# A Fourier-matrix aside rank of six instead of three, and a search over three hundred orders instead of ninety, in an attention and Fourier-mixing kernel

## The chip, the cores and the metric

The kernel runs on one core of one Trainium2 chip. Its time is the device time of one execution in microseconds (us). Before the change three runs took 2828.16, 2829.85 and 2834.0 us, so the median is 2829.85 us.

## The reference, cut to what matters

```python
# A: attention, 32 heads of 32, S = 2048, D = 1024, full softmax
qkv = (x @ wqkv).reshape(B, S, 3, 32, 32).transpose(2, 0, 3, 1, 4)
scores = einsum("bhqd,bhkd->bhqk", q, k) * 32 ** -0.5
o = einsum("bhqk,bhkd->bhqd", softmax(scores), v)
a = o.transpose(0, 2, 1, 3).reshape(B, S, D) @ wo
# B: Fourier mixing, real part of DFT_seq(DFT_hidden(x))
re, im = einsum("bsd,ed->bse", x, hid_re), einsum("bsd,ed->bse", x, hid_im)
y = einsum("ts,bse->bte", seq_re, re) - einsum("ts,bse->bte", seq_im, im)
return concatenate([a, y], axis=-1)
```

The kernel first multiplies B's x by the sequence matrices (cosine `ct[0]`, then sine `ct[1]`, the second Fourier matrix) and then by the hidden ones.

## The kernel before

**Work of the matrix engine.** Every float32 product outside attention is made of three matmuls of 128x128 by 128x512: both operands are split into a high and a low part (a "piece", `halves`, lines 535 to 548: a cast on ACT or DVE, L542 or L544, and a subtraction on POOL or DVE, L547), and high*high, low*high and high*low are added up in one PSUM bank. On top of that the products follow a seven-product scheme, so pieces are sums or differences of blocks (line 522 makes such a sum from two loads). All these matmuls (line 457) are called fills; there are 6528 of them. Attention runs beside them, head by head: scores in pairs of matmuls (L1896, tile `psS`), whose row maxima DVE takes (L1902) and whose exponentials ACT sums (L1905); the scores transposed (L2018, tile `psT`), whose exponentials ACT writes as `pt` (L2022); and `pt` times v (L2037, "PV"), 20 or 24 matmuls of each of 96 PV steps.

**What sets the order.** The program first only records operations, each with an engine (sometimes a second engine it could go to), a rank, what it waits for and which buffer of a ring it takes. A planner (`Plan`, `run`) then walks through a modelled time with costs per operation. For ACT, DVE, POOL and SP it takes the ready operation with the lowest rank; for PE it chooses between the next fill (in the one fixed order of `fills`) and the next step of scores, transposed scores and PV. The rank is mostly `seq()`, the number of product groups recorded so far, plus 10, 20 or 25 for an operation's second choice. What comes out is each engine's fixed list of instructions. On the chip each engine goes down its list and waits at each instruction for that one's inputs.

**The search.** Eight numbers steer the choices (LATE, NEAR, PATIENCE, STOCK, SFIRST, SST, LEAD, RES). The planner is run once with set values, then TRIALS times with drawn ones: every third time a fresh draw, otherwise the best so far with two numbers redrawn; a draw is kept if the modelled end is earlier. The best is then emitted. The seed is fixed.

**Pieces made aside.** Some pieces of the two big products with the sequence matrices are made early, beside the projection of q, k and v, and stored to DRAM (`ha_d`) for later. `aside_c` (line 1306) makes such pieces of B's x from loads `c<-in_xb` (L1327): a sum (L1333), a cast (L1334), a subtraction (L1335) and two stores (L1336). It makes 16, eight each for two products, and gives all their operations `rank = seq() + LATER`. `aside` makes others, among them sums of blocks of the Fourier matrices (loads L1373 `slot<-in_ct`, sum L1375, store L1381 `tg_d`, `tb_d`), at `seq() + AHEAD`, and the change leaves that rank alone. While q, k and v are projected, aside pieces, loads for the projection (L506: `raw<-in_wqk`, `raw<-tx_d`) and the first heads share SP's one list of DMA issues.

```python
pp, p, i = todo_c.pop(0)
rank = seq() + LATER
...
for n in range(TRIALS):
    if n % 3 == 0:
        some = {k: rng.uniform(*v) for k, v in SPAN.items() if rng.random() < 0.6}
    else:
        some = {**best, **{k: rng.uniform(*SPAN[k]) for k in rng.sample(list(SPAN), 2)}}
    t = run(True, **some)
    if t < shortest:
        best, shortest = some, t
```

Of the kernel before, what the change touches and what calls it, by code (L numbers as in the profile page):

```python
# [253 lines left out]
def kernel(  # L254
# [137 lines left out]
    LATE = 0.25  # L392
    HB = 0
    ACAST = 0.6
    TRIALS = 90
    RES = 700
    SST = 13
    LEAD = 3.0
# [901 lines left out]
    def put_b(r, pp, j):  # L1300
        return pp, "b", r, j
# [37 lines left out]
    kept_a = {}  # L1339

    todo_a = [put_b(1, pp, j) for pp in ORDER if pp in (5, 6, 7, 4) for j in range(16)]
    AHEAD, EACH, LATER = 2, 1, 3

    todo_t = [put_b(0, 4, j) for j in range(16)]

# [843 lines left out]
    best, shortest = {}, run(True)  # L2189
    for n in range(TRIALS):  # L2190
        if n % 3 == 0:
# [41 lines left out]
```

## Time and profile before

| | before |
|---|---|
| median of three runs | 2829.85 us |
| the profiled execution | 2831.55 us |
| its span (first to last instruction) | 2829.8 us |
| PE busy | 2797.1 us (99%), 14728 matmuls |
| DVE busy | 2377.2 us (84%) |
| ACT busy | 2355.6 us (83%) |
| POOL busy | 1191.7 us (42%) |
| DMA, mean | 271 GB/s |

PE is the matrix engine, DVE VectorE, ACT ScalarE, POOL GpSimd, SP SyncE, which issues nearly all DMAs. A PE that is shown busy isn't always at its full pace: a matmul lasts about 380 ns in the profile while the next may start 216 ns after it, so that a pause up to some 160 ns between two starts isn't shown as idle. An idle time in brackets stands with the instruction that ended it and with what it had waited for.

### The profile page before, as it was taken

The page shows a single profiled execution, that of the slowest core. Times are in us where ns is not written, and L with a number is a line of the kernel's source. Part 1 is how long each engine was busy: PE and PEld are TensorE (multiplying, and loading weights), DVE is VectorE, ACT ScalarE, POOL GpSimd, SP SyncE. Part 2 cuts the span into 40 slices and gives each one's busy share as a digit, 9 for nine tenths or more (in the row PEclk, how much of TensorE's full clock was granted, in tenths as well). Part 3 has the DMA queues.
Part 4 walks back from the last instruction along what each step waited for, and adds up shares of the span by engine and source line. Part 5 has one row for each costly group of instructions (what it writes and reads, how often), then busy time and mean ns, then how long its engine had stood idle before and what let it go on. Part 6 is the DMA issues. An engine that isn't in the chain of part 4 may idle for free.

```text
span 2829.8 us, 47069 instructions
## 1 busy us (share of the span) xinstructions
PE 2797.1 (99%) x14728; PEld 2095.6 (74%) x14728; DVE 2377.2 (84%) x3300; ACT 2355.6 (83%) x4490; POOL 1191.7 (42%) x945
## 2 busy tenths in 40 slices
PE   9999999999999999999999999999999999999999
PEld 8787777776777777677676777767767777777777
DVE  6678888788888888798988899888888998888845
ACT  5348898998899899889999988999988988888851
POOL 2234434133234432356545446676765331343300
PEclk9999999999999999999999999999999999999999
DMA  9989978798899988977999767888867665677548
GB/s 345 344 312 305 316 249 293 252 337 298 300 302 344 333 298 297 296 232 231 335 342 339 251 207 241 293 270 266 277 179 237 220 211 185 203 237 252 178 154 296
DMA packets 485844, 768.18 MB, mean 271 GB/s; under 512 B 120382, under 2 KB 153406, under 8 KB 485470
## 3 DMA queue, kind: packets, MB, share of 16 engines
q1 hardware_dynamic: 485452, 765.04, 81.6%
q8 instruction: 119, 1.95, 0.3%
q14 instruction: 129, 1.06, 0.1%
q10 hardware_dynamic: 144, 0.13, 0.0%
HBM read 511.74 MB, written 253.25 MB: 270 GB/s over the span
## 4 chain that ended last, share of the span: by engine, by line
PE 88%; DMA 5%; ACT 3%; DVE 2%; issue 1%; POOL 1%; SPq 1%; DVEq 0%; POOLq 0%; ACTq 0%
PE pd L457 40%; PE pd L2037 15%; PE psT L2018 15%; PE psS L1896 14%; PE psT L457 4%; ACT psS L1905 2%; ACT pt L2022 1%; DVE negm L1902 1%; DMA ha_d<-slot 1%; DMA ha_d<-c 0%; DMA c<-in_xb 0%; DMA raw<-in_xa 0%; DMA slot<-in_ct 0%; DMA qs<-qk_d 0%; DMA raw<-in_wv 0%
## 5 line engine op out<-in xcount | busy, mean ns | idle before, releaser
L457 PE MATMUL pd<-slot,hl 128*128 128x512 f32 x5088 | 1412.1, 380 | 4.0 <-ACT hl L542 2.0
L2022 ACT ACTIVATE pt<-psT 128x512 f32<-128x512 f32 x2048 | 1215.3, 689 | 228.8 <-PE psT L2018 227.3
L1902 DVE TENSOR_REDUCE negm<-psS 128x1 f32<-128x1024 f32 x1024 | 1241.5, 1219 | 169.2 <-PE psS L1896 153.8
L1905 ACT ACTIVATE psS<-psS,negm 128x1024 f32<-128x1024 f32 x1024 | 1225.1, 1197 | 41.6 <-DVE negm L1902 40.7
L457 PEld LDWEIGHTS pd<-slot,hl 128*128 128x128 f32 x5088 | 963.8, 190 | 133.3 <-ACT hl L542 2.4
L2018 PE MATMUL psT<-qs,ks 128*128 128x512 f32 x2048 | 786.0, 387 | 1.2 <-DMA r_d<-ll 0.7
L2018 PEld LDWEIGHTS psT<-qs,ks 128*128 128x128 f32 x2048 | 383.2, 188 | 168.8 <-issue 46.9
L1896 PE MATMUL psS<-ks,qs 128*128 128x512 f32 x1552 | 457.9, 381 | 9.1 <-ACT psS L1905 8.9
L2037 PE MATMUL pd<-pt,vt 128*32 128x512 f32 x4096 | 459.3, 594 | 2.8 <-DVE e L766 1.8
L547 POOL TENSOR_TENSOR slot<-raw,slot 128x512 fp32r<-128x512 f32 x153 | 194.9, 1279 | 353.8 <-DVE slot L547 98.8
L547 POOL TENSOR_TENSOR slot<-slot,slot 128x512 fp32r<-128x512 f32 x206 | 260.4, 1280 | 196.3 <-DVE slot L544 50.1
L1896 PEld LDWEIGHTS psS<-ks,qs 128*128 128x128 f32 x1552 | 283.7, 189 | 66.4 <-ACT psS L1905 21.3
L2037 PEld LDWEIGHTS pd<-pt,vt 128*32 128x32 f32 x4096 | 123.9, 110 | 281.4 <-issue 261.3
L1905 ACT ACTIVATION_READ_ACCUMULATOR psS<-psS,negm 128x1 f32 x1024 | 324.8, 317 | 0.0
L522 POOL TENSOR_TENSOR raw<-raw,g 128x512 f32<-128x512 f32 x114 | 145.4, 1279 | 231.9 <-DMA g<-tg_d 23.6
L547 POOL TENSOR_TENSOR hl<-raw,hl 128x512 fp32r<-128x512 f32 x113 | 144.4, 1279 | 214.8 <-PE psT L2018 62.0
L457 PE MATMUL pd<-slot,slot 128*128 128x512 f32 x780 | 200.8, 379 | 0.0
L457 PEld LDWEIGHTS pd<-slot,slot 128*128 128x128 f32 x780 | 147.4, 189 | 20.1
L1896 PE MATMUL psS<-ks,qx 128*128 128x512 f32 x496 | 146.5, 386 | 6.1 <-ACT psS L1905 5.3
L1896 PEld LDWEIGHTS psS<-ks,qx 128*128 128x128 f32 x496 | 90.0, 189 | 34.9 <-ACT psS L1905 10.9
L522 DVE TENSOR_TENSOR raw<-raw,g 128x512 f32<-128x512 f32 x146 | 106.9, 740 | 9.1 <-issue 2.2
L2050 DVE TENSOR_TENSOR ot<-ot,pd 128x512 f32<-128x512 f32 x64 | 43.9, 686 | 68.7 <-PE pd L2037 67.9
(139 smaller groups left out, 2135.0 us busy)
## 6 DMA issues: line engine op xcount, KB each, us to landing
hl<-ha_d SPq DMA_DIRECT2D x134, 512.0 KB
slot<-in_ct SPq DMA_DIRECT2D x144, 256.0 KB
qk_d<-e SPq DMA_DIRECT2D x52, 512.0 KB
qs<-qk_d SPq DMA_DIRECT2D x128, 192.0 KB
ks<-qk_d SPq DMA_DIRECT2D x128, 192.0 KB
raw<-g_d SPq DMA_DIRECT2D x96, 256.0 KB
ha_d<-hl SPq DMA_DIRECT2D x42, 512.0 KB
raw<-in_ct SPq DMA_DIRECT2D x80, 256.0 KB
```

Source lines behind the costliest of these rows:

```text
L457: nc.tensor.matmul(box["ps"], a[1]((a[0].hi, a[0].lo)[u]()), turns((b[0].hi, b[0].lo)[v]()), start=k == 0, stop=k == n - 1)
L522: (nc.gpsimd if e == "POOL" else nc.vector).tensor_tensor(out=dest(), in0=dest() if a is None else a.get(), in1=other["q"] if "q" in other ...
L547: (nc.gpsimd if e == "POOL" else nc.vector).tensor_tensor(out=lo(), in0=raw(), in1=f(hi()), op=ALU.subtract)
L1896: nc.tensor.matmul(p[:, i * NB : i * NB + NB], (QX[0] if own else QS[h % 2])[:, qt * P : qt * P + P], turns(KS[h % 2][:, c * 1024 + i * NB ...
L1902: nc.vector.tensor_reduce(out=ST["negm"][:, c, qt : qt + 1], in_=box["p"], axis=AX.X, op=ALU.max, negate=True)
L1905: nc.scalar.activation(box["p"], box["p"], AF.Exp, bias=ST["negm"][:, c, qt : qt + 1], accum_out=ST["sums"][:, c, qt : qt + 1])
L2018: nc.tensor.matmul(box["p"], KS[h % 2][:, t * P : t * P + P], turns(QS[h % 2][:, j * NB : j * NB + NB]), start=True, stop=True)
L2022: nc.scalar.activation(box["t"], box["p"], AF.Exp)
L2037: nc.tensor.matmul(po["p"][j * DH : j * DH + DH, :], VT[h][:, k, :], box["t"], start=(k == t0), stop=(k == t), tile_position=(0, j * DH),)
L2050: nc.vector.tensor_tensor(out=as_two(po["o"]), in0=as_two(po["o"]), in1=order_of(po["p"]), op=ALU.add)
```

## The change

Two constants change. The pieces that `aside_c` makes rank six groups behind the place where they are recorded, not three; and the search goes on to 300 draws.

```diff
-    TRIALS = 90
+    TRIALS = 300
...
-    AHEAD, EACH, LATER = 2, 1, 3
+    AHEAD, EACH, LATER = 2, 1, 6
```

No operation is added or removed and no cost or limit of the planner changes, yet the lists of all five engines come out otherwise, since the search keeps other numbers. The counts of PE's matmuls stay (6528 fills, 2048 scores, 2048 transposed scores, 96 PV steps). Some operations change engine: of the sums on line 1375 DVE has 47 and not 41, of those on line 858 (sums for the projection, from a load `c<-u_d`) 4 and not 2, and all in all DVE has 17 instructions fewer, ACT 22 more and POOL 5 fewer. If only TRIALS is raised and LATER stays three, the lists are those of before, row for row; the rank of six with 90 draws gives lists that differ from both. Up to about 48 us the lists are the same, and from about 100 to 180 us they are again, but for two or three rows.

**Three places of it.** The first is PE's list in head 7's stretch of the sine product (3312 fills done; at 1363 to 1371 us before). Before, after the last three fills:

```order
L457 MATMUL pd<-slot_15934,hl 128x512 x3
L1896 MATMUL psS<-ks_2705,qs_2704 128x512 x2
L2018 MATMUL psT<-qs_709,ks_710 128x512 x2
L1896 MATMUL psS<-ks_2705,qs_2704 128x512 x2
L2018 MATMUL psT<-qs_709,ks_710 128x512 x2
L1896 MATMUL psS<-ks_2705,qs_2704 128x512 x2
L2018 MATMUL psT<-qs_709,ks_710 128x512 x2
L1896 MATMUL psS<-ks_2705,qs_2704 128x512 x2
L2018 MATMUL psT<-qs_709,ks_710 128x512 x2
L2037 MATMUL pd<-pt,vt 32x512 x20
```

And now:

```order
L457 MATMUL pd<-slot_15953,hl 128x512 x3
L1896 MATMUL psS<-ks_2705,qs_2704 128x512 x2
L2018 MATMUL psT<-qs_709,ks_710 128x512 x2
L1896 MATMUL psS<-ks_2705,qs_2704 128x512 x2
L2018 MATMUL psT<-qs_709,ks_710 128x512 x2
L1896 MATMUL psS<-ks_2705,qs_2704 128x512 x2
L2018 MATMUL psT<-qs_709,ks_710 128x512
L2037 MATMUL pd<-pt,vt 32x512 x20
L2018 MATMUL psT<-qs_709,ks_710 128x512 x2
L1896 MATMUL psS<-ks_2705,qs_2704 128x512 x4
```

Scores follow transposed scores with no fill between them three times before PV there, and now two times; eleven fills further up the new list has one such place that the old one lacks. Over the whole list, without those right behind a PV step, which every head has, there were 14 such places and are now 15. Pairs of transposed scores with no fill between them, counted in the same way, were 26 and are now 23.

The second place is SP's list of DMA issues at about 228 to 236 us, with the buffers' numbers: `c_2804` is an aside piece of x, `slot` with `in_ct` are blocks of the Fourier matrix, `raw_2964` and `raw_2983` (now `raw_2962` and `raw_2975`) blocks for the next projection group. Before:

```order
L1373 DMA slot13_2856<-in_ct 128x512
L1336 DMA ha_d2_5_1_292<-c_2804 128x512
L1381 DMA tg_d5_1_0_421<-slot12_2811 128x512
L1336 DMA ha_d2_5_1_292<-c_2886 128x512
L1327 DMA c_2804<-in_xb 128x512
L1381 DMA tg_d5_1_1_422<-slot14_2841 128x512
L1373 DMA slot12_2926<-in_ct 128x512 x2
L1381 DMA tg_d5_1_2_423<-slot13_2856 128x512
L1373 DMA slot14_2948<-in_ct 128x512 x2
L506 DMA raw_2964<-tx_d1_514 128x512
L1373 DMA slot13_2976<-in_ct 128x512
L506 DMA raw_2983<-in_wqk 128x512
```

And now:

```order
L1373 DMA slot13_2855<-in_ct 128x512
L1381 DMA tg_d5_1_0_421<-slot12_2811 128x512
L1336 DMA ha_d2_5_1_292<-c_2804 128x512
L1336 DMA ha_d2_5_1_292<-c_2887 128x512
L1373 DMA slot12_2915<-in_ct 128x512 x2
L1327 DMA c_2804<-in_xb 128x512
L1381 DMA tg_d5_1_1_422<-slot14_2841 128x512
L1381 DMA tg_d5_1_2_423<-slot13_2855 128x512
L506 DMA raw_2962<-tx_d1_514 128x512
L1373 DMA slot14_2969<-in_ct 128x512
L506 DMA raw_2975<-in_wqk 128x512
```

Between the common first row and the load of the projection's weights (`raw_2983`, now `raw_2975`) stood five loads of Fourier blocks; now there are three, two of them ahead of the aside load. The rest of the stretch is the same seven transfers in another order, so that two transfers of 256 KB fewer stand ahead of that load.

The third is ACT's list there: the casts of those two blocks (`slot5`, `hl`) among the exponentials of head 0 (`sums_1458`) and the first of head 1. Before:

```order
L1905 ACTIVATE psS_2951,sums_1458<-psS_2951,negm_1457 128x1024
L1905 ACTIVATE psS_2980,sums_1458<-psS_2980,negm_1457 128x1024
L1905 ACTIVATE psS_2997,sums_1458<-psS_2997,negm_1457 128x1024
L542 ACTIVATE slot5_3026<-raw_2964 128x512
L542 ACTIVATE hl_3038<-raw_2983 128x512
L1905 ACTIVATE psS_3020,sums_1458<-psS_3020,negm_1457 128x1024
L1905 ACTIVATE psS_3032,sums_3031<-psS_3032,negm_3030 128x1024
L1961 ACTIVATE tt_3068<-tt_3068 128x32
L1334 ACTIVATE c_2804<-c_2797 128x512
```

And now:

```order
L542 ACTIVATE slot4_2982<-raw_2773 128x512
L1905 ACTIVATE psS_2955,sums_1458<-psS_2955,negm_1457 128x1024
L1905 ACTIVATE psS_2987,sums_1458<-psS_2987,negm_1457 128x1024
L542 ACTIVATE slot5_3021<-raw_2962 128x512
L1905 ACTIVATE psS_3007,sums_1458<-psS_3007,negm_1457 128x1024
L542 ACTIVATE hl_3040<-raw_2975 128x512
L1334 ACTIVATE c_2804<-c_2797 128x512
L1905 ACTIVATE psS_3025,sums_1458<-psS_3025,negm_1457 128x1024
L542 ACTIVATE e_3069<-e_3053 128x512
L542 ACTIVATE slot6_3073<-raw_2995 128x512
L1905 ACTIVATE psS_3050,sums_3049<-psS_3050,negm_3048 128x1024
```

The two casts stood together ahead of two exponentials; now one exponential is between them, and the cast of the aside piece (L1334) has moved from behind head 1's first exponential to ahead of head 0's last.

## Rows read from the trace of the kernel before

**Rows 1.** Which the page's head and its list of busy time give
```profile
span 2829.8 us, 47069 instructions
...
PE 2797.1 (99%) x14728; PEld 2095.6 (74%) x14728; DVE 2377.2 (84%) x3300; ACT 2355.6 (83%) x4490; POOL 1191.7 (42%) x945
```

**Rows 2.** Stretches: length, then busy time and count per engine, TensorE's granted clock, DMA
```profile
0.00:100.00 100.00, 98.54 (x442) 85.53 (x443) 71.36 (x105) 48.87 (x83) 22.20 (x21) 1.00 0.98 344
100.00:200.00 100.00, 95.45 (x430) 81.90 (x430) 67.52 (x97) 37.19 (x62) 27.50 (x22) 0.98 0.99 345
200.00:300.00 100.00, 96.66 (x458) 75.35 (x460) 88.87 (x115) 84.26 (x157) 52.61 (x41) 0.98 0.88 291
700.00:800.00 100.00, 100.00 (x537) 74.70 (x540) 87.41 (x134) 89.80 (x174) 32.12 (x25) 1.00 0.84 284
2800.00:2829.80 29.80, 23.05 (x107) 19.84 (x105) 12.90 (x20) 0.00 (x0) 0.00 (x0) 0.95 0.92 327
```

**Rows 3.** What the matrix engine waited for: sum, times, longest (us)
```profile
PE psS L1896 <- ACT psS L1905: 14.2, 23, 2.6
PE pd L457 <- ACT hl L542: 2.0, 1, 2.0
PE pd L2037 <- DVE e L766: 1.8, 1, 1.8
```

**Rows 4.** Timeline of PE, 1362 to 1373 us: start, duration, instructions, idle before
```profile
1363.37 1.03 PE L457 MATMUL pd<-slot,hl 128*128 128x512 f32 x4
...
1365.70 0.70 PE L1896 MATMUL psS<-ks,qs 128*128 128x512 f32 x2 [0.44 <-ACT psS L1905]
...
1367.77 0.70 PE L1896 MATMUL psS<-ks,qs 128*128 128x512 f32 x2 [0.61 <-ACT psS L1905]
```

**Rows 5.** Timeline of PE, 100 to 140 us
```profile
119.02 0.48 PE L457 MATMUL pd<-slot,hl 128*128 128x512 f32 x1 [1.99 <-ACT hl L542]
...
128.46 2.64 PE L457 MATMUL psT<-slot,hl 128*128 128x512 f32 x11 [1.27 <-DVE hl L547]
...
134.87 2.64 PE L457 MATMUL pd<-slot,hl 128*128 128x512 f32 x11 [0.96 <-POOL hl L547]
```

**Rows 6.** Timeline of PE, 235 to 252 us
```profile
242.69 0.88 PE L1896 MATMUL psS<-ks,qx 128*128 128x512 f32 x2 [2.57 <-ACT psS L1905]
```

**Rows 7.** Timeline of ACT, 235 to 245 us
```profile
238.43 0.63 ACT L542 ACTIVATE slot<-raw 128x512 fp32r<-128x512 f32 x1 [1.36 <-DMA raw<-tx_d]
240.91 0.63 ACT L542 ACTIVATE hl<-raw 128x512 fp32r<-128x512 f32 x1 [1.85 <-DMA raw<-in_wqk]
241.45 1.07 ACT L1905 ACTIVATE psS<-psS,negm 128x1024 f32<-128x1024 f32 x1
```

**Rows 8.** Stretches around two waits, columns as in rows 2
```profile
243.10:246.50 3.40, 3.40 (x10) 2.69 (x9) 1.99 (x2) 3.40 (x9) 1.01 (x1) 0.50 0.84 288
246.50:250.00 3.50, 3.50 (x18) 3.07 (x17) 3.03 (x8) 2.77 (x5) 1.29 (x1) 1.00 0.36 131
484.50:488.00 3.50, 3.50 (x36) 1.32 (x40) 2.98 (x4) 0.76 (x2) 0.63 (x1) 1.00 1.03 266
```

**Rows 9.** DMA issues of SyncE, 228 to 238 us
```profile
229.52 0.93 SPq L1373 DMA_DIRECT2D slot<-in_ct  x2
...
232.66 0.81 SPq L1373 DMA_DIRECT2D slot<-in_ct  x2
233.56 0.38 SPq L506 DMA_DIRECT2D raw<-tx_d  x1
...
235.49 0.42 SPq L506 DMA_DIRECT2D raw<-in_wqk  x1
```

**Rows 10.** Timeline of PE, 1140 to 1146 us
```profile
1144.16 0.70 PE L1896 MATMUL psS<-ks,qs 128*128 128x512 f32 x2 [1.60 <-ACT psS L1905]
```

**Rows 11.** Timeline of DVE, 1138 to 1144 us
```profile
1140.39 0.69 DVE L1375 TENSOR_TENSOR slot<-slot 128x512 f32<-128x512 f32 x1 [1.92 <-DMA slot<-in_ct]
...
1141.60 2.34 DVE L1902 TENSOR_REDUCE negm<-psS 128x1 f32<-128x1024 f32 x2
```

## The prediction

> **What bounds the kernel now.** I read the page's head first. The matrix engine is busy 2797.1 of 2829.8 us [rows 1], and the change neither adds nor removes one of its matmuls. So only the 32.7 us in which it is idle, and the stretches in which it runs below its pace, can move. The view by stretches says where they are [rows 2]: 1.46 us before and among the first matmuls, 4.55 us between 100 and 200 us, 3.34 us between 200 and 300 us, nothing in many later stretches (700 to 800 us stands for them), and 6.75 us at the end, behind the last matmul. That leaves 32.7 - 1.46 - 4.55 - 6.75 = 19.9 us after 200 us, 3.34 of it in a single stretch.
>
> The waits of the matrix engine come next [rows 3]. The largest entry is scores (L1896) waiting for the exponentials of the pair two before them, 14.2 us in 23 waits. The rest are single waits of 1 to 2 us. Then I looked at these places in the timeline, and found two kinds.
>
> The first kind is in the order itself. Where the next fill's operands aren't there in time by the planner's reckoning, it alternates scores and transposed scores with no fill between, and the engine then goes at ACT's pace. Two scores pairs start at 1365.70 and 1367.77 us [rows 4], 2.07 us apart, with four matmuls in that turn, the pair and two transposed ones. At full pace, four fills from 1363.37 to 1364.24 us are 0.87 us (they last 1.03 us, the last one's overlap of 0.16 us taken off). Such a turn thus costs 2.07 - 0.87 = 1.2 us.
>
> The second kind the planner did not foresee: an engine's list is stopped by an instruction whose load came late, and attention's work stands behind it. Between 100 and 200 us the fills wait three times for pieces (1.99, 1.27, 0.96 us) [rows 5]. At 242.69 us the scores wait 2.57 us [rows 6], because ACT's list has two casts for the next projection group ahead of the exponential: the first waits for `raw<-tx_d` until 238.43 us, the second for `raw<-in_wqk` until 240.91 us, and only then, at 241.45 us, does the exponential begin that frees the bank [rows 7].
>
> The second kind has a further price. From 243.10 to 246.50 us the granted clock is 0.50, the lower of the two levels, 1.2 GHz, with 10 matmuls in 3.4 us, against 18 in 3.5 us in the next stretch at 1.00 [rows 8]. Half of 3.4 us is lost, 1.7 us. The wait of 2.57 us thus cost 4.3 us in all. The PV step that begins at about 484.5 us had waited 1.8 us for DVE's `e` [rows 3], and behind it the clock stays at 1.00 [rows 8].
>
> **The change part by part.** *The start.* The lists of all engines from about 100 to 180 us come out as before but for a few rows; the three waits of 4.2 us together stay. Cost 0; bounds -4.2 (all go) and +2.
>
> *The wait at 242 us.* In SP's list two transfers of 256 KB fewer stand ahead of the load for which the second cast waits. In the stretch from 200 to 300 us DMA moves 291 GB/s at a share of 0.88 [rows 2], so 524,288 bytes are 1.8 us. The issues say the same by another way: the weights' load is issued at 235.49 us, behind two pairs of Fourier blocks at 229.52 and 232.66 us and the projection's block at 233.56 us [rows 9]; without the second pair, which waited for its store, it may go about 2 us earlier. I take 1.8 us of the 2.57 us, which leaves 0.8 us. ACT's list also has one exponential between the two casts now, so that less of attention stands behind the late one; against that, the aside piece's cast now stands ahead of head 0's last exponential. Its sum needs the aside load, which now goes out behind a pair of Fourier blocks (0.93 us of issuing [rows 9]). Both count as nothing, with 0.9 us to either side.
>
> *The clock there.* A wait of 0.8 us is shorter than the one of 1.8 us after which the clock stayed up [rows 3, 8]. So I take the half-clock stretch as gone as well: -1.7 us, with 0 as the other bound. The Trainium skill, "TensorE: Matmul & The Clock Gate", section "HAM oscillation — how this bites in real kernels", says that a matrix engine which sits idle for long enough falls to half its clock and then runs its next work slowly until it has been busy again. The rows at 243 us agree (0.50 after 2.57 us idle). By that rule a new wait of this length, wherever the new order makes one, brings its own slow stretch, so it speaks against a change that redraws every wait: with one new wait the sum would be 1.7 us worse than by the wait alone.
>
> *The starved turns.* Scores behind transposed scores without a fill: 14 places before, 15 now. One more at 1.2 us: +1.2 us. Turns that end after the second transposed one, with no scores behind, become fewer, 12 to 8 (26 pairs of transposed scores less the 14, 23 less the 15); I count them at nothing, with -1 us as the bound. These stalls are in the order itself, so nothing hides them.
>
> *Sums that change engine.* DVE does 47 of the sums of Fourier blocks and not 41, and 4 of the sums on L858 and not 2. Such a sum takes 0.69 us on DVE and hides beside the matrix engine as long as its load has landed. If it hasn't, DVE stops: at 1140.39 us the sum begins after 1.92 us of idle time for `slot<-in_ct`, and the row maxima behind it begin at 1141.60 us [rows 11]. Then ACT is late, and the scores wait 1.60 us, until 1144.16 us [rows 10]. It is the one long wait of this kind among the 41. At one in 41, eight more cost 8/41 x 1.6 = 0.3 us, which I leave out; bounds -1.6 (that one wait goes) and +8 x 1.6 = 12.8 us.
>
> *The search.* Two hundred and ten more draws cost nothing on the chip. At rank three they change no row, so they act only together with the rank of six. What they give is the order that the points above have counted.
>
> *The sum.* -1.8 - 1.7 + 1.2 = -2.3 us. The profiled execution of before took 2831.55 us, 1.75 us around its span and 1.7 us over the median of 2829.85 us. It would become 2829.2 us, and the median 2829.85 - 2.3 = 2827.5 us.
>
> **The rivals.** *The gain is given back.* Every list after 200 us is new, and new late loads can stop it elsewhere. For: DMA is busy 0.88 to 0.99 of the time in the first 300 us [rows 2], and it is the loads' landing that the planner misjudges. Against: the counts of sums and casts by engine are nearly the same. One new wait like that at 242 us is 2.57 + 1.7 = 4.3 us, which gives 2827.5 + 4.3 = 2831.8 us.
>
> *More of the waits go.* Of the 19.9 us idle after 200 us, the 14 turns show about 0.55 us each as idle (0.44 and 0.61 us [rows 4]), 7.7 us. The other 12.2 us are waits of the second kind. If half of the 9.6 us left without that at 242 us go too, it is 4.8 us more, 2822.7 us; if the turns also get fewer than their places say, since a load lands early, down to 2820 us. For: the aside loads now yield to three more groups of the projection of q, k and v, whose pieces the fills wait for first. Against: the first aside loads stand at the same rows of SP's list as before.
>
> *Slower: aside sums on DVE that stop the row maxima.* The place is DVE's list where it makes these sums, the price 1.60 us a wait [rows 10] and 1.7 us where one is long enough to take the clock down [rows 8]. Five more such waits, one of them with the clock, are 5 x 1.6 + 1.7 = 9.7 us; with -2.3 us that is 2837.3 us. It decides from the second such wait on (2 x 1.6 exceeds 2.3). For: eight more such sums on DVE. Against: one in 41 until now, and DVE is busy 84% in all.
>
> *The change does not do what it says.* The rank alone may matter to no wait, since the order of the first six aside pieces is as before; then all is redrawn by the search and comes out level, 2829.85 us.
>
> **How the numbers follow.** My forecast 0.43, with an own range of 2824 to 2831 us; given back 0.20; more waits gone 0.20; slower 0.12; no effect 0.05. The range that should hold the time 8 times in 10 goes from 2820 us (most of the second rival) to 2835.5 us (the lower part of the slower one). A measurement of this kernel tells no change from one of 0.2%, 5.7 us, so faster means below 2824.2 us and slower above 2835.5 us. Faster: 0.15 of the forecast's chance and most of the second rival, 0.06 + 0.18 = 0.24, about 0.25. Slower: 0.10 of its own and 0.03 of the case in which the gain is given back more than once, 0.13. The rest, 0.62, is no change.
>
> **What would show it.** Right, if scores at about 240 us wait under 1 us, the granted clock between 200 and 300 us is 1.00, PE's waits between 100 and 200 us stand as before, and the scores' waits for exponentials sum to about 13 us (14.2 - 1.8 + 0.6). Wrong, if a wait of more than 2 us for the scores or a PV step stands at a new place with a half-clock stretch behind it, or if sums on L1375 on DVE are found waiting for `in_ct` ahead of row maxima. A matrix engine with fewer than 25 us idle would mean the second rival.

## The result, and the profile after

The changed kernel takes 2838.76 us (median of 19 runs, 2832.46 to 2847.70), the kernel before 2829.58 us beside it (19 runs, 2824.89 to 2834.01). The ratio is 1.0030 with an interval of 1.0024 to 1.0037: slower by 0.3%, 8.5 us, outside the predicted range. The profiled execution of the changed kernel took 2842.6 us, that of before 2831.55 us; so the two traces differ by 11 us, the medians by 9.2 us.

The page's head of the changed kernel, beside [rows 1]:

```profile
span 2840.8 us, 47069 instructions
...
PE 2799.3 (99%) x14728; PEld 2100.0 (74%) x14728; DVE 2377.3 (84%) x3283; ACT 2370.7 (83%) x4512; POOL 1189.1 (42%) x940
```

PE does the same work and is idle for 2840.8 - 2799.3 = 41.5 us, not 32.7. Where, the view by stretches says (length, busy time and count of PE, PEld, DVE, ACT, POOL, granted clock, DMA share and GB/s). After:

```profile
100.00:200.00 100.00, 95.30 (x430) 81.82 (x429) 66.91 (x97) 37.37 (x63) 27.51 (x21) 0.98 0.98 343
200.00:300.00 100.00, 97.39 (x482) 76.86 (x481) 88.82 (x116) 85.49 (x159) 58.28 (x46) 1.00 0.92 310
200.00:700.00 500.00, 495.98 (x2616) 374.17 (x2615) 428.68 (x579) 445.51 (x851) 210.14 (x165) 1.00 0.87 294
700.00:1100.00 400.00, 395.69 (x2119) 292.18 (x2118) 339.89 (x458) 357.01 (x684) 140.42 (x111) 1.00 0.91 308
1100.00:1600.00 500.00, 487.79 (x2588) 350.15 (x2587) 438.46 (x614) 450.93 (x863) 248.77 (x198) 1.00 0.86 285
1600.00:2700.00 1100.00, 1091.46 (x5854) 808.76 (x5856) 966.03 (x1330) 980.46 (x1881) 536.46 (x425) 1.00 0.73 232
```

The kernel before, in the same long stretches:

```profile
200.00:700.00 500.00, 492.69 (x2584) 366.85 (x2583) 430.03 (x581) 438.19 (x835) 198.29 (x156) 1.00 0.87 290
700.00:1100.00 400.00, 400.00 (x2151) 299.78 (x2150) 344.63 (x471) 359.93 (x693) 145.87 (x115) 1.00 0.92 313
1100.00:1600.00 500.00, 493.46 (x2635) 356.81 (x2634) 445.14 (x626) 455.10 (x874) 253.32 (x201) 1.00 0.87 292
1600.00:2700.00 1100.00, 1093.93 (x5868) 806.45 (x5871) 957.75 (x1330) 974.98 (x1873) 543.25 (x431) 1.00 0.73 231
```

There is a gain and a loss. From 200 to 700 us PE gains 3.3 us of work; the prediction had looked at the first 100 us of this stretch. From 700 to 1600 us it loses 4.3 + 5.7 = 10.0 us, and 2.5 us after that. Before, the profile shows no idle time of PE for 400 us. In the prediction's own count, idle time after 200 us and up to the last matmul, the 19.9 us of before are now 29.1 us. PE's waits, beside [rows 3]:

```profile
PE psS L1896 <- ACT psS L1905: 19.1, 29, 1.9
PE pd L457 <- ACT hl L542: 2.2, 1, 2.2
PE psT L2018 <- DMA qs<-m_d: 2.0, 1, 2.0
...
PE pd L2037 <- DVE slot L1171: 1.4, 1, 1.4
```

The scores wait 19.1 us and not 14.2, with six more waits. Four of PE's longest waits at new places, in its timeline (start, duration, instructions, idle before; [rows 6, 10] are their like):

```profile
225.99 0.70 PE L1896 MATMUL psS<-ks,qs 128*128 128x512 f32 x2 [1.78 <-ACT psS L1905]
...
818.32 1.06 PE L2037 MATMUL pd<-pt,vt 128*32 128x512 f32 x8 [1.38 <-DVE slot L1171]
...
1128.32 0.70 PE L1896 MATMUL psS<-ks,qs 128*128 128x512 f32 x2 [1.63 <-ACT psS L1905]
...
1565.65 0.79 PE L1896 MATMUL psS<-ks,qs 128*128 128x512 f32 x2 [1.92 <-ACT psS L1905]
```

What stood in front of attention's work there, on ACT (beside [rows 7]) and then on DVE (beside [rows 11]):

```profile
224.21 0.63 ACT L542 ACTIVATE hl<-raw 128x512 fp32r<-128x512 f32 x1 [2.18 <-DMA raw<-in_wqk]
```

```profile
816.97 0.69 DVE L522 TENSOR_TENSOR raw<-raw,g 128x512 f32<-128x512 f32 x1 [2.23 <-DMA g<-in_ct]
817.58 0.68 DVE L1171 COPY slot<-pd 128x512 f32<-128x512 f32 x1
...
1125.14 0.69 DVE L1375 TENSOR_TENSOR slot<-slot 128x512 f32<-128x512 f32 x1 [2.64 <-issue]
1125.75 2.35 DVE L1902 TENSOR_REDUCE negm<-psS 128x1 f32<-128x1024 f32 x2
...
1561.88 0.69 DVE L522 TENSOR_TENSOR slot<-slot,slot 128x512 f32<-128x512 f32 x1 [1.12 <-DMA slot<-in_ct]
1562.48 0.68 DVE L2050 TENSOR_TENSOR ot<-ot,pd 128x512 f32<-128x512 f32 x1
1563.08 2.35 DVE L1902 TENSOR_REDUCE negm<-psS 128x1 f32<-128x1024 f32 x2
```

Each is the picture of [rows 7] or [rows 11] at a new place: an instruction is late, and a row maximum or an evacuation stands behind it. Three of the four waited for a load by the profile; for the sum at 1125.14 us it names no cause ("issue"). That this one waited for its load too is inferred from the kernel before. The sums on L1375 between 980 and 1200 us come one by one, each with its two loads and its store, and by its place among them (the seventh from the last, 2819 fills done) the one at 1125.14 us was on POOL before (2823 fills done), where it waited for `slot<-in_ct`. The sixth from the last, [rows 11]'s sum on DVE, is now on POOL. Before and after, in POOL's timeline:

```profile
1125.64 1.28 POOL L1375 TENSOR_TENSOR slot<-slot 128x512 f32<-128x512 f32 x1 [5.55 <-DMA slot<-in_ct]
...
1138.11 1.29 POOL L1375 TENSOR_TENSOR slot<-slot 128x512 f32<-128x512 f32 x1 [3.32 <-DMA g<-so_d]
```

If these are the same sums, one that changed engine brought the wait at 1128.3 us, and another took away the one at 1144.2 us [rows 10].

To compare orders I split PE's lost time in three, from the starts of all its matmuls: by how much a start lies further behind the one before than the pace allows (216 ns; a PV step's own pace), where that is over 0.05 us. "Turns" are scores or transposed scores directly behind transposed scores, which the planner lays down itself; "half clock" is what stretches at 0.50 add outside PV steps; "unforeseen" is the rest, half clock inside PV steps included (about 6 us of it in e7). The end behind the last matmul, 4 to 7 us, is in none of the three. The columns are of one profiled execution each, and these stood 3.5 us below to 7.8 us above their kernel's median. The last column tells how long DVE stood still for loads (0.3 us or more at a time, from 190 to 2680 us) while PE was not in a PV step.

| order | median, us | ratio to before, 95% | turns | unforeseen | half clock | DVE's stalls outside PV |
|---|---|---|---|---|---|---|
| before | 2829.58 | | 23.3 | 33.8 | 3.1 | 5.7 |
| before, again (e12) | 2831.29 | 1.0003 (0.9994 to 1.0012) | 23.3 | 31.9 | 1.4 | 4.8 |
| changed | 2838.76 | 1.0030 (1.0024 to 1.0037) | 22.8 | 43.9 | 4.4 | 21.6 |
| changed, again (e11) | 2837.35 | 1.0025 (1.0014 to 1.0037) | 22.8 | 43.8 | 3.1 | 20.8 |
| e1 rank 6, before's numbers | 2845.74 | 1.0060 (1.0047 to 1.0074) | 28.9 | 43.4 | 3.8 | 10.1 |
| e2 rank 3, changed kernel's numbers | 2847.96 | 1.0057 (1.0043 to 1.0071) | 32.2 | 40.1 | 4.5 | 17.7 |
| e3 rank 6, 90 draws | 2843.87 | 1.0044 (1.0032 to 1.0057) | 23.8 | 46.2 | 1.4 | 20.2 |
| e4 rank 3, e3's numbers | 2846.38 | 1.0058 (1.0045 to 1.0072) | 28.0 | 46.2 | 4.2 | 17.7 |
| e5 rank 3, long slack | 2849.52 | 1.0075 (1.0062 to 1.0087) | 27.7 | 49.9 | 1.5 | 10.4 |
| e6 rank 3, short slack | 2839.16 | 1.0036 (1.0024 to 1.0049) | 22.9 | 38.2 | 4.8 | 15.9 |
| e7 rank 3, set numbers | 2845.09 | 1.0056 (1.0044 to 1.0069) | 27.2 | 47.5 | 4.0 | 11.8 |
| e8 rank 6, set numbers | 2842.66 | 1.0044 (1.0030 to 1.0057) | 32.1 | 37.8 | 3.5 | 12.1 |
| e9 changed, 8 moved | 2835.06 | 1.0020 (1.0010 to 1.0031) | 22.8 | 49.1 | 0.0 | 21.6 |
| e10 before, 6 moved | 2827.55 | 0.9996 (0.9987 to 1.0006) | 23.1 | 29.0 | 2.2 | 1.9 |
| e13 changed, all moved | 2840.04 | 1.0034 (1.0022 to 1.0045) | 23.0 | 43.5 | 1.5 | 4.2 |
| e14 before, 4 stalls put in | 2833.13 | 1.0011 (1.0000 to 1.0021) | 23.2 | 35.9 | 3.8 | 6.7 |

Of the 11 us between the first two traces, the turns give -0.5, the unforeseen waits +10.1 and the half clock +1.3. Between the second executions they give -0.5, +11.9 and +1.7, 13.1 us in all, of which an end shorter by 2.4 us (4.1 us in e11, 6.4 in e12) gives some back: the two stand 10.1 us apart.

### The profile page after: what moved, and what is told of

It is laid out like the page before. It is cut to its first block, busy times and chain, and to the rows that moved or that the text cites. A ratio compares the mean times of both kernels' runs of the same rounds, so it can differ in the third digit from the quotient of the medians.

```text
span 2840.8 us, 47069 instructions
## 1 busy us (share of the span) xinstructions
PE 2799.3 (99%) x14728; PEld 2100.0 (74%) x14728; DVE 2377.3 (84%) x3283; ACT 2370.7 (83%) x4512; POOL 1189.1 (42%) x940
## 4 chain that ended last, share of the span: by engine, by line
PE 50%; DMA 5%; ACT 3%; DVE 2%; SPq 1%; issue 1%; POOL 1%; DVEq 0%; POOLq 0%; ACTq 0%
PE pd L457 23%; PE pd L2037 9%; PE psT L2018 9%; PE psS L1896 8%; ACT psS L1905 2%; ACT pt L2022 1%; PE psT L457 1%; DVE negm L1902 1%; DMA slot<-in_ct 1%; DMA yo_d<-slot 1%; DMA ha_d<-slot 1%; DMA m_d<-lt 0%; DMA si_d<-slot 0%; DMA slot<-tg_d 0%; DMA tb_d<-slot 0%
## 5 line engine op out<-in xcount | busy, mean ns | idle before, releaser
L457 PE MATMUL pd<-slot,hl 128*128 128x512 f32 x5112 | 1429.8, 380 | 5.0 <-ACT hl L542 2.2
L547 POOL TENSOR_TENSOR slot<-slot,slot 128x512 fp32r<-128x512 f32 x199 | 252.2, 1280 | 219.1 <-DVE slot L544 64.9
L1905 ACT ACTIVATION_READ_ACCUMULATOR psS<-psS,negm 128x1 f32 x1024 | 314.8, 307 | 0.0
L522 POOL TENSOR_TENSOR raw<-raw,g 128x512 f32<-128x512 f32 x121 | 157.2, 1302 | 221.4 <-issue 27.1
L522 DVE TENSOR_TENSOR raw<-raw,g 128x512 f32<-128x512 f32 x139 | 103.3, 750 | 20.0 <-DMA raw<-in_wd 3.9
L2050 DVE TENSOR_TENSOR ot<-ot,pd 128x512 f32<-128x512 f32 x64 | 43.9, 685 | 62.4 <-PE pd L2037 61.8
```

Of the source, the lines that this page charges most:

```text
L457: nc.tensor.matmul(box["ps"], a[1]((a[0].hi, a[0].lo)[u]()), turns((b[0].hi, b[0].lo)[v]()), start=k == 0, stop=k == n - 1)
L522: (nc.gpsimd if e == "POOL" else nc.vector).tensor_tensor(out=dest(), in0=dest() if a is None else a.get(), in1=other["q"] if "q" in other ...
L547: (nc.gpsimd if e == "POOL" else nc.vector).tensor_tensor(out=lo(), in0=raw(), in1=f(hi()), op=ALU.subtract)
L1905: nc.scalar.activation(box["p"], box["p"], AF.Exp, bias=ST["negm"][:, c, qt : qt + 1], accum_out=ST["sums"][:, c, qt : qt + 1])
L2050: nc.vector.tensor_tensor(out=as_two(po["o"]), in0=as_two(po["o"]), in1=order_of(po["p"]), op=ALU.add)
```

## The experiments

**Rank or numbers?** The first four fix what the search chose, and exchange it between the ranks.

```diff
-    TRIALS = 300
+    TRIALS = 0
...
-    best, shortest = {}, run(True)
+    best, shortest = {"LATE": 0.1766, "RES": 566.6}, run(True)   # e1, rank 6: what the kernel before kept
+    # e2, rank 3: LATE 0.2036, NEAR 0.3035, PATIENCE 0.4887, STOCK 1.771, RES 558.5, LEAD 4.80, what the changed one kept
+    # e3, rank 6: LATE 0.2036, NEAR 0.3035, PATIENCE 0.4711, STOCK 1.995, RES 732.0, LEAD 3.008, what 90 draws keep
+    # e4, rank 3: the numbers of e3
```

> Rank six with the planner's numbers that the order of before uses (LATE 0.177, RES 567), no search: the rank alone. If the rank itself costs the time, about 2838 us. If the numbers kept by the longer search cost it, about 2830 us. If each order only draws its waits for late loads anew and before had a lucky draw, anywhere from 2830 to 2842 us, with starved turns at 23 us as in both profiles and the difference to before in the other waits of the matrix engine (33.8 us in before, 43.9 us in the changed kernel).

> Rank three with the eight numbers that the changed kernel uses, no search: the numbers alone. Rank theory: about 2830 us. Numbers theory: about 2838 us. Redraw theory: 2830 to 2842 us, not tied to either, and likelier above 2834 than below.

> Rank six with the numbers that 90 draws keep (those of draw 80): half of the change, without the 210 further draws. If the further draws did the harm, about 2830 us; if the rank did it, about 2838 us; redraw theory: 2830 to 2842 us.

> Rank three with the numbers of draw 80, the partner of the run before. Rank theory: 8 us faster than its partner, about 2830 us. Redraw theory: it differs from its partner by up to 8 us with either sign.

Measured: 2845.74, 2847.96, 2843.87 and 2846.38 us, all slower than both kernels, and all above the 2842 us up to which the expectation of a redraw had gone. Neither half of the change carries the loss alone: before's numbers with rank six cost 16 us, the changed kernel's numbers with rank three 18 us. The further 210 draws did no harm at rank six (2843.87 to 2838.76 us; the intervals of the two ratios just overlap). Where the numbers are the same, rank six is 16 us slower (e1), 9 us faster (the changed kernel and e2) or not told apart (e3 and e4, 2.5 us): the rank has no sign of its own.

**Set numbers, and the slack for loads.** The planner reckons a load's user ready 2.0 us after the load's modelled landing.

```diff
-    SLACK = {("SP", "POOL"): 2.0, ("SP", "DVE"): 2.0, ...}
+    SLACK = {("SP", "POOL"): 3.5, ("SP", "DVE"): 3.5, ...}   # e5; e6: 1.0; both rank 3, 90 draws
...
+    TRIALS = 0    # e7 (rank 3) and e8 (rank 6): the code's set numbers, no draw, slack 2.0
```

> Rank three, 90 draws, and the planner counts a load as usable by DVE, ACT and POOL 3.5 us after it lands, not 2.0 us. Theory of late loads: the matrix engine's waits that the planner did not foresee fall from 34 to 46 us to under 30 us, while starved turns (scores behind transposed scores with no fill: 20 places, 14 before) rise by some 6 to 10 us above 23 us; the time is 2830 to 2840 us. If those waits have another cause than loads that land after the planner's time, they stay at 40 to 46 us and the time is above 2845 us.

> The same with 1.0 us in place of 2.0 us, rank three, 90 draws. Theory of late loads: unforeseen waits above 50 us, starved turns (16 places) about 22 us, time above 2845 us. Other cause: unforeseen waits 34 to 46 us as in the six orders so far and, since the planner sees fewer starved turns, a time of 2830 to 2840 us.

> Rank three with the eight numbers as they stand in the code, no draw at all: one more order that no search has picked. Redraw theory: unforeseen waits 40 to 46 us, 18 starved places, 2843 to 2850 us. If rank three as such were the good one, below 2835 us.

> Its partner at rank six, no draw: 22 starved places. Redraw theory: unforeseen waits 40 to 46 us, 2845 to 2852 us, within 8 us of its partner. If the rank itself cost 9 us, 9 us above its partner.

Measured: the long slack 2849.52 us, with DVE's stalls outside PV steps down to 10.4 us but unforeseen waits of 49.9 us; the short slack 2839.16 us, with 38.2 us. Both go against the theory that the unforeseen waits are loads that land later than the slack allows (under 30 us and over 50 us were expected); but each slack also drew a new order, so they do not rule it out. With set numbers the two ranks are not told apart (2.4 us), and e8 came out below its expected range in time and in waits. By now eight orders that are neither kernel's took 2839.16 to 2849.52 us, none of them faster than the changed kernel. Five of the eight (e1, e2, e4, e7, e8) use numbers that no search kept for their rank, and pay 4 to 9 us more in turns; so the fair measure is the column of unforeseen waits, 37.8 to 49.9 us. In it the changed order (43.9 us) is an ordinary one and the order of before (33.8 and 31.9 us) the lowest. From 700 to 1100 us this is plain: PE is busy 391.7 to 398.0 us of 400 in those eight, and 400.00 only in the order of before. From 1100 to 1600 us the changed order is poor even beside them: 487.8 us of 500, and 485.8 us when executed again below, against 487.5 to 492.1 us in the eight and 493.5 us before. The worst of the eight from 700 to 1100 us, e3:

```profile
700.00:1100.00 400.00, 391.68 (x2088) 285.65 (x2087) 330.75 (x452) 350.40 (x672) 147.29 (x116) 1.00 0.90 303
```

**The stalled instructions moved, in an order that is otherwise kept.** The next kernels record the planned order and emit it with single instructions moved down their engine's list (with what depends on them in between). Their line numbers are 2 lower than the kernel's. An entry is engine, place in its list, and by how many places.

```diff
-    run(False, **best)
+    run(True, **best)
+    for e, at, by in MOVES:
+        ...
+        todo[a:b + 1] = [x for x in todo[a:b + 1] if x not in late] + late
+    for o, e, d, (att_on[0], t_on[0]) in todo:
+        o.emit(e) if o.other else o.emit()
+ # e9, changed kernel: (ACT 149 1) (ACT 1767 1) (ACT 1769 2) (DVE 882 2) (DVE 980 2) (DVE 981 2) (DVE 1224 1) (DVE 1729 2)
+ # e10, before: (ACT 161 1) (ACT 162 2) (DVE 356 3) (DVE 369 1) (DVE 531 2) (DVE 1250 2)
+ # e11, changed kernel, and e12, before: none
```

> The changed kernel's order, with eight instructions moved a step or three down their engine's list and nothing else: at 224 us ACT's cast of the projection's weights goes behind the next exponential; at 817, 904 (two of them), 1125 and 1562 us DVE's sum of two loaded blocks goes behind the evacuation and the row maximum that stood behind it; at 1455 and 1457 us two of ACT's casts of summed Fourier blocks go behind the next exponentials. The same loads land as late, and no load moves. Theory (an engine's list stops at a late load, and attention's work behind it is what the matrix engine then lacks): the matrix engine's waits at 226.0, 818.3, 908.6, 1128.3, 1456.7, 1458.7 and 1565.7 us (1.78, 1.38, 1.23, 1.63, 0.48, 0.87 and 1.92 us, 9.3 us in all) go nearly all, and with the one at 1565.7 us the half-clock stretch behind it, 1.7 us. That is 11.0 us; if 7 to 11 of it stay gone, the kernel takes 2828 to 2832 us, about the time of the kernel before. Rival (the waits are a sign of transfers or of ACT's work being short; what is gained at one place is waited for at the next): 2836 to 2839 us, with new waits close behind the old places.

> The kernel before, with six instructions moved down their engine's list in the same way: at 238 and 241 us ACT's two casts, each behind an exponential that stood behind it; at 340 us DVE's cast of an aside piece behind the next row maximum; at 352 us its sum of an aside piece, and at 481 us a sum of two loaded blocks, behind the evacuation that PV waits for; at 1140 us the sum of Fourier blocks behind an evacuation and a row maximum. Theory: the waits at 242.7, 344.5, 353.6 and 1144.2 us (2.57, 0.69, 0.84 and 1.60 us) go, about half of the 1.78 us at 484.4 us, and the half-clock stretch at 243 us (1.7 us): 8.3 us, so 2821 to 2824 us, faster than both kernels. Rival (waited for elsewhere): 2828 to 2830 us, no change.

Measured: e9 2835.06 us, 2 to 4 us below the changed kernel's medians, with overlapping intervals, and not the 7 to 11 expected. In its profile the waits at the moved places are gone or shorter, but others of 0.9 to 1.7 us stand at 974.9, 1056.5, 1138.2, 1212.7 and 1389.7 us; the unforeseen waits sum to 49.1 us (that execution, 2842.83 us, was near the top of its 12). e10 took 2827.55 us, the lowest median of all, but its interval holds 1: 2.2 us below the runs beside it, 3.7 us at most by the interval, and not the 6 to 8 expected. It beats the changed kernel; that it beats the kernel before is not shown. That these waits as such are what is lost was borne out in neither. Whether the new ones come from the moves or from the execution, the controls tell:

> The changed kernel's lists row for row, emitted from the recorded order (no instruction moved): the control for the two runs with moved instructions, and a second profiled execution of the same order. Theory (the waits are in the order): 2836 to 2841 us; the waits over 0.5 us stand at the same places as in the first profile, at 226.0, 818.3, 908.6, 1128.3, 1565.7 and 1830.4 us among them, each within 0.3 us. Rival (the landing of a load differs from execution to execution, and an order only decides how many places are exposed to it): the same median, but of those six waits behind late loads two or more are gone or shorter by over 0.5 us, and others of 1 us or more stand where the first profile has none, while waits without a load behind them (711.4, 1105.7, 2054.1, 2304.9 us) repeat within 0.1 us.

> The kernel before's lists row for row, emitted in the same way: what the comparison tells from no change, and a second profiled execution. Theory: 2829 to 2831 us, waits at 242.7, 353.6, 484.4 and 1144.2 us as before within 0.3 us. Rival: the same median within 2 us (0.1%), with one or more of 242.7, 353.6 and 1144.2 us shorter by over 0.5 us, and others new; 484.4 us and the turns without a fill repeat.

Measured: 2837.35 and 2831.29 us. PE's timeline in the second execution of the changed order:

```profile
226.23 0.70 PE L1894 MATMUL psS<-ks,qs 128*128 128x512 f32 x2 [1.40 <-ACT psS L1903]
...
817.01 3.21 PE L2035 MATMUL pd<-pt,vt 128*32 128x512 f32 x28 [0.31 <-DVE slot L1169]
...
1127.52 0.70 PE L1894 MATMUL psS<-ks,qs 128*128 128x512 f32 x2 [1.66 <-ACT psS L1903]
...
1145.13 0.48 PE L2016 MATMUL psT<-qs,ks 128*128 128x512 f32 x1 [1.53 <-ACT pt L2020]
...
1568.13 0.70 PE L1894 MATMUL psS<-ks,qs 128*128 128x512 f32 x2 [1.33 <-ACT psS L1903]
```

Single waits come and go: 1.38 us at 818 us became 0.31 us, 1.92 at 1566 us became 1.33, and 1.53 us at 1145 us is new. In two executions of each order the sums repeat: unforeseen waits 43.9 and 43.8 us in the changed order, 33.8 and 31.9 us in that of before (idle time after 200 us 29.1 and 28.6 us against 19.9 and 18.5); and so do the stretches. In the second execution of before, and then of the changed kernel:

```profile
700.00:1100.00 400.00, 400.00 (x2148) 298.19 (x2147) 341.46 (x470) 359.89 (x692) 146.26 (x116) 1.00 0.93 313
1100.00:1600.00 500.00, 495.42 (x2648) 360.17 (x2647) 448.34 (x628) 457.95 (x880) 253.90 (x201) 1.00 0.88 294
```

```profile
700.00:1100.00 400.00, 396.53 (x2123) 294.11 (x2122) 340.77 (x458) 357.74 (x686) 141.59 (x111) 1.00 0.92 309
1100.00:1600.00 500.00, 485.83 (x2579) 349.45 (x2578) 437.69 (x613) 448.52 (x860) 246.37 (x196) 1.00 0.86 284
```

So most of what is lost belongs to the order, while the place varies from one execution to the next; that the loads' landing decides it is the likely reading. DVE's stalls showed a difference that repeats as well: before, 12 to 17 of 17 to 22 us lie beside PV steps, when the matrix engine needs no row maximum at once; after, 13 of 34.5 us. Is that the cause, or a sign? e13 moves every such instruction of the changed order (22 on DVE, 3 on ACT) behind the next row maximum; e14 puts stalls in front of row maxima in the order of before.

```diff
+ # e13: the moves of e9, and (DVE 530 1) (922 1) (932 1) (934 1) (976 1) (1065 1) (1150 1) (1167 1) (1231 1) (1240 2) (1247 1) (1306 1) (1526 1) (1603 1) (1610 2) (1682 2) (1695 1)
+ # e14, row maxima behind the sums that follow them: (DVE 845 1) (DVE 1302 1) (DVE 1617 1) (DVE 1715 1)
```

> The changed kernel's order; wherever DVE stood still for a load by 0.3 us or more outside a PV step in either of its two profiles (22 places; in both profiles DVE's stalls for loads outside PV steps sum to about 21 us, in the kernel before to about 5 us), the waiting instruction goes behind the next row maximum, and ACT's three casts go behind the next exponentials as in the ninth run. Theory (those stalls, by what stands behind them, are the loss): unforeseen waits of the matrix engine fall from 43.8 us to 33 to 36 us, 2828 to 2831 us. Rival (the stalls' places are a sign only: the loads are late for the pieces too, and the fills then wait, or ACT's pace does): they stay above 40 us, 2834 to 2838 us, with waits of fills (L457 in the kernel, for POOL's or DVE's pieces) grown by 3 us or more.

> The kernel before's order, with four row maxima moved behind the sum that follows them in DVE's list and that waits for its load: three beside a PV step (before that sum DVE stood still 1.24, 2.06 and 2.53 us, at 772.5, 1190.9 and 1529.5 us) and one outside of PV steps (1.38 us, at 1447.0 us). Theory (a stall costs only where the matrix engine needs what stands behind it within about 2 us; beside a PV step of 4.5 us it doesn't): at the first three places the matrix engine waits 0.7 us or less, at the fourth 1.3 to 2.5 us; 2831 to 2833 us. Rival (a stalled list costs its stall wherever it is): 1.2 to 2.5 us at each of the four, 2836 to 2838 us.

Measured: e13 took 2840.04 us, 2 us above the rival's range. DVE's stalls outside PV steps fell from about 21 to 4.2 us, and the unforeseen waits stayed at 43.5 us. PE's waits in it:

```profile
PE psS L1894 <- ACT psS L1903: 15.5, 28, 1.5
PE pd L455 <- POOL slot L545: 3.1, 3, 1.3
PE pd L455 <- POOL hl L545: 2.9, 2, 1.7
...
PE psT L2016 <- ACT pt L2020: 2.1, 1, 2.1
```

The scores wait 15.5 and not 19.1 or 18.1 us, and the fills wait 6.0 us for POOL's pieces where the two profiles of the changed order have 1.9 and 2.5 us. So the stalls in front of row maxima are a sign, as the rival says: without them as much is lost. Its further step, that moving a sum makes the fill wait instead, is not shown. In e9 the late instructions in front of three of these fills (two sums and a cast on DVE) stand unmoved, and there the fills wait 0.89, 0.94 and 1.21 us (974.9, 1212.7 and 1389.7 us), in e13 1.33, 1.18 and 1.70 us. PE's waits in e9:

```profile
PE pd L455 <- POOL slot L545: 2.4, 3, 0.9
PE pd L455 <- POOL hl L545: 2.2, 2, 1.2
```

e14: 2833.13 us, 2.4 us over the runs beside it (the interval starts at 1.0000), just above the theory's range and below the rival's. Its four places in PE's timeline, where there is a wait at all:

```profile
1195.30 0.70 PE L1894 MATMUL psS<-ks,qx 128*128 128x512 f32 x2 [0.82 <-ACT psS L1903]
...
1451.07 0.70 PE L1894 MATMUL psS<-ks,qs 128*128 128x512 f32 x2 [0.79 <-ACT psS L1903]
```

At 773 us DVE stood still 2.35 us in front of the row maximum, beside a PV step, and the scores behind it waited for nothing; nor did those behind the stall of 1.89 us at 1530 us. Behind the 3.49 us at 1192 us they waited 0.82 us, a little over the 0.7 us expected. Outside of PV steps, behind 1.39 us at 1447 us, the wait was 0.79 us, less than the 1.3 to 2.5 expected. At these four places stalls of 9.1 us cost 1.6 us.

Lighter loads in the same order were not tried: the instructions behind them would read parts of a buffer that nothing has written. Not tried either were the changed order with its sums given back to the engines of before, and one engine's list of before among the others' of after.

## Why the prediction was wrong, point by point

- *The start*: right. PE is busy 95.30 us between 100 and 200 us, 95.45 before [rows 2].
- *The wait at 242 us and the clock there*: both went, as forecast (97.39 us busy from 200 to 300 us at a clock of 1.00). But two other half-clock stretches came, at 1566.1 and 2074.7 us, and the same pattern, an ACT cast waiting for `raw<-in_wqk` in front of an exponential, came back 17 us earlier with 1.78 us (1.40 us in the second execution). So before 300 us 2.57 + 1.7 became 1.78 us, a gain of 2.5 and not 3.5 us.
- *The starved turns*: forecast +1.2 us, measured -0.5 us (23.3 to 22.8), so 1.7 us off and with the wrong sign. The turns that end after the second transposed one became fewer, and the sum had counted them at nothing, with -1 us as the bound.
- *Sums that change engine*: named, and counted at nothing. Of the five long waits after 700 us behind a stalled sum (818.3, 908.6, 1128.3, 1458.7 and 1565.7 us), two stand behind L1375, three behind L522, which the prediction did not look at. One of the two, at 1128.3 us, is by its place behind a sum that went from POOL to DVE, which was one of the prediction's own signs of being wrong; another sum that went the other way took the wait of [rows 10] with it, so that these two about cancel. For the one at 1458.7 us it is not known. Prices of 0.9 to 1.9 us fit the 1.60 us of [rows 10].
- *The search*: "nothing of itself" holds at rank three. At rank six the medians differ by 5.1 us in favour of the 210 further draws (e3 against the changed kernel), with intervals that just overlap.
- *The step that failed is the sum*: it took the waits that the planner did not foresee, apart from the one at 242 us, as carried over, though every list after 200 us was new. In -1.8 - 1.7 + 1.2 no term stands for new waits; only the rivals have them. Measured, the unforeseen waits rose by 10.1 us (11.9 between the second executions), and the 19.9 us idle after 200 us to 29.1 us, where the sum leaves about 18.7 (19.9 - 1.8 + 0.6). (The 12.2 us "of the second kind" are less than the split's 33.8 us because they are idle time after 200 us alone; the split also counts what lies before and pauses that the profile shows as busy.) The stretch from 700 to 800 us, quoted as one where nothing is lost [rows 2], was, looking back, the warning: where no wait is left, a new order can only lose, and eight other orders lose there too. The change lost 4.3 us from 700 to 1100 us and 5.7 us in the 500 us behind.
- *The rivals*: "given back" had the mechanism and counted it once, at 4.3 us. "Slower" had five waits and 2837.3 us, near the 2838.76 measured, with a chance of 0.12; but in e13 those stalls in front of row maxima are nearly gone and the time stays lost, and the two sums whose change of engine is seen to matter about cancel. That the number came out close is luck.

Shown: the loss is in waits outside the starved turns, from 700 to 1600 us above all, it repeats as a sum and not place by place, and the eight other orders that were tried have waits of this kind too, more than that of before. Not shown: what makes the order of before lose so little there. DVE's stalls in front of row maxima are not it by themselves (e13); against the loads' slack e5 and e6 speak, without ruling it out.

## What to carry to other kernels

When a change redraws a whole order, price the redraw itself: look for the stretches in which the old order is at its best, and build and time a few neighbours (another rank, another draw) before reading a reason out of single places; here eight of them lay 10 to 20 us above the old one, and the changed one was no worse than the best of them. A place at which a trace shows a wait behind a late load can be gone in the next execution; compare sums over two executions of the same lists. Moving the stalled instructions aside is no sure gain: the loads are late for the pieces as well.

## What the hardware showed that I had not expected

The prediction took half-clock stretches for the price of one long wait, with [rows 8] on its side. The profiles show that, and also long waits without such a stretch and such a stretch without a long wait. In the second execution of before, 0.50 begins 0.4 us before the end of a wait of 2.77 us, and again not at one of 1.79 us at 483 us:

```profile
240.53 1.22 PE L1894 MATMUL psS<-ks,qx 128*128 128x512 f32 x2 [2.77 <-ACT psS L1903]
...
483.26 1.06 PE L2035 MATMUL pd<-pt,vt 128*32 128x512 f32 x8 [1.79 <-DVE e L764]
```

```profile
240.10:243.50 3.40, 2.97 (x7) 2.43 (x8) 1.23 (x1) 3.40 (x9) 1.84 (x2) 0.50 1.04 390
482.00:487.00 5.00, 3.74 (x36) 1.44 (x40) 4.24 (x6) 2.08 (x5) 1.92 (x2) 1.00 0.95 269
```

In e13 the clock stays at 1.00 behind a wait of 2.09 us at 1142.8 us, but falls at 1500 us:

```profile
1142.82 0.48 PE L2016 MATMUL psT<-qs,ks 128*128 128x512 f32 x1 [2.09 <-ACT pt L2020]
```

```profile
1142.80:1146.20 3.40, 3.38 (x16) 2.98 (x17) 1.18 (x3) 3.31 (x7) 2.06 (x2) 1.00 0.80 298
1500.00:1503.40 3.40, 3.40 (x9) 2.68 (x10) 2.74 (x8) 3.18 (x8) 1.26 (x1) 0.50 1.08 349
```

In front of that one PE had no long wait, only two starved turns of 0.61 us idle each (e13, PE's timeline):

```profile
1497.75 0.70 PE L1894 MATMUL psS<-ks,qx 128*128 128x512 f32 x2 [0.61 <-ACT psS L1903]
...
1499.82 1.10 PE L1894 MATMUL psS<-ks,qx 128*128 128x512 f32 x2 [0.61 <-ACT psS L1903]
```

The same, two or three such turns, stands in front of the stretches at 2074.7 us in the changed kernel, 1366.0 us in e10 and 1134.5 us in e14. They need not: behind the two turns of [rows 4] (0.44 and 0.61 us idle) the profile shows no such stretch. So starved turns can cost 1.7 us beside their own 1.2 us each, which the sum of the prediction left out. The Trainium skill, "TensorE: Matmul & The Clock Gate", section "HAM oscillation — how this bites in real kernels", ties the lower level to an engine that sits idle for long enough; these rows agree in part only, since here it also fell after matmuls that were merely sparse.

One order's executions also differ by more than I had allowed for: the changed kernel's 19 runs span 15.2 us, those of before 9.1 us, and a profiled execution stood 3.8 us from its median (the changed kernel) or 7.8 us (e9).
